# Attention and an MLP mixer on one core: where finished tiles are turned and sent, in the first and in the last batch element

## The chip, the cores and the metric

The kernel runs on one core of one Trainium2 chip. The metric is the device time of one execution in microseconds (us), the median of three runs. A profile of one execution is taken beside it; its span runs from the first to the last instruction.

## The reference

Eight batch elements go through attention with normalised queries and keys (12 heads, 448 tokens, 64 columns a head), and the result of each, 448 tokens by 768 channels, goes through an MLP mixer.

```python
# attention, per head
q_n, k_n = rmsnorm(q, g_q), rmsnorm(k, g_k)
scores = (1 / sqrt(64)) * q_n @ k_n.T
attn = softmax(scores)                      # max taken off, sum + 1e-9
x[b, :, head columns] = attn @ v            # x: (8, 448, 768)
# mixer
h = maximum(x.transpose(0, 2, 1) @ w_tok1, 0) @ w_tok2      # 448 -> 256 -> 448 tokens
u = x + h.transpose(0, 2, 1)
h2 = maximum(u @ w_ch1, 0) @ w_ch2                          # 768 -> 1536 -> 768 channels
out = u + h2                                                # float32
```

The reference computes in float32; the weights can arrive as 64-bit numbers and are converted on the chip.

## The kernel before

One instruction stream is written per engine: the order of the calls is the order on each engine, and an engine waits where its next instruction needs a result or a buffer. The work is cut into small items (a cost in us and a function); `merge` interleaves lists of items by their costs, and `run` emits them. `later(us, fn)` emits `fn` once so many us of item cost have gone by.

The result of an element is kept channel by token (`uT`: six tiles of 128 channels by 448 tokens). To be stored it is turned in blocks of 32 by 32 on VectorE into a tile of `turn_pool` (four buffers), and four transfers, one for each 32 channels, take it to the output:

```python
turn_pool = pool("turn_pool", 4)
r_pool = pool("r_pool", 1)
...
def send_y(b, cc, t):
    dst = out[b][:, cc * P:(cc + 1) * P]
    for i in range(0, P, 32):
        (nc.sync if in_next(b) else nc.scalar).dma_start(
            out=dst[:, i:i + 32].rearrange("(n t) c -> t n c", t=32),
            in_=t[i:i + 32].rearrange("t (n c) -> t n c", c=32))
...
def trans_y(b, cc):
    t = st["y", cc] = turn_pool.tile([P, S], F32, name="turned")
    nc.vector.transpose(out=t[:], in_=st["uT", b][:, cc, :])

def turns(b, cs, send=True):
    def one(cc):
        trans_y(b, cc)
        if send:
            later(2.0, lambda: send_y(b, cc, st.pop(("y", cc))))
    return [(0.3, lambda cc=cc: one(cc)) for cc in cs]

def y_order(b):
    return [o * KC + m for m in ((0, 1, 2) if b else (2, 0, 1)) for o in range(2)]

def in_next(b):                 # this element's tiles are sent inside the next element
    return b < B - 1 and not shifted
```

Element 0 computes the channel MLP in `first_stage` with plain products, 36 stages of 8 matmuls (18 for each layer), while the weights are still being converted on VectorE (`weight_items`: L264, L265, L267, L282, L309) and stored to DRAM. For elements 1 to 7 sums of weight blocks are made on GpSimd (`sum_items`: L205 to L208, loads L241 `raw<-ws`, stores L212 `ws<-raw`), and `ch1` and `ch2` use seven products in place of eight, with weights loaded as units (L740 `unit<-ws`).

```python
def first_stage(n):
    ...
    if t == 0:
        st["m", 0], st["m", 1] = m_tile(), m_tile()        # two PSUM banks, and there are two
    a, u = st.pop(("stage", n)), st["uT", 0]
    for o in range(2):
        ps = st["m", o][:, 0:S]
        ...                                                # matmuls, L781
        if t < last:
            continue
        if wide:                                           # second layer
            to, c = u[:, o * KC + m, :], r_tile(1 + o)[:]
            nc.scalar.copy(out=c, in_=ps)                                    # L790
            nc.gpsimd.tensor_tensor(out=to, in0=to, in1=c, op=ALU.add)       # L791
        else:
            nc.scalar.activation(out=natural(o)[:, :, m, :], ..., func=AF.Relu)
```

Three more places matter. `x_items(0, h)` turns half `h` of element 0's attention result on TensorE (L663) and ScalarE copies it to SBUF (L665); `tok1` multiplies it (L685, with ScalarE's relu L688), `tok2` follows (L693), and VectorE adds its bank to `uT` (L698). Attention for element b+1 runs between these items: scores (L385), exponentials on ScalarE (L389), values (L459), sums (L427), row scales (a square on ScalarE L1170 or L1173, a reduce on VectorE L1187, then L1195 to L1230), and turned queries and keys (L350, L365, L368). The last of the denominators' products with an element's values is L505 on VectorE, its factor turned by L502.

```python
def first_items(tok, prods, some):
    ...
    for j, it in enumerate(prods[:-6]):
        items.append(it)
        ...
        if j in (26, 28):
            items += turns(0, [y_order(0)[j // 2 - 13]])
    return items, prods[-6:]

def last_items(b):
    single = [(us(6, HS), lambda i=i: ch2(b, 1, i, 0)) for i in range(7)]
    l = turns(b, y_order(b)[:4], not in_next(b))
    return [single[0]] + merge(single[1:-1], l) + [single[-1]]
...
for b in range(B):
    early, double = middle_items(b)
    if b == 0:
        early, last = first_items(tok1_items(0, 0) + x_items(0, 1) + tok1_items(0, 1) + early, double, some)
    else:
        if b > 1 and in_next(b - 1):
            y, z = sends(b - 1, y_order(b - 1)[:4]), left
            left = [y[0], y[1], z[0], y[2], z[1], y[3]]
        run(merge(tok1_items(b, 0), left[:2]))
        begin, early = merge(tok1_items(b, 1) + early[:3 * KC], left[2:]), early[3 * KC:]
        ...
    if b == 0:
        last = x_items(1, 1) + merge(last, direct + sums[:5], turns(b, y_order(b)[2:4]))
    else:
        ...
        last += last_items(b)
    run(merge(att, early) + last)
    if b == 0:
        load_units(0)
    left = turns(b, y_order(b)[4:])
run(left)
```

In `ch2` of group 1, the last one, products 0 to 6 (`single`) add into the last channel tiles 2 and 5: tile 2 has its last add at product 5, tile 5's second half at product 4, and tile 5's first half at product 6, the last of all.

Of the kernel before, what the change touches and what calls it, by code (L numbers as in the profile page):

```python
# [8 lines left out]
F32 = mybir.dt.float32  # L9
# [4 lines left out]
ALU = mybir.AluOpType  # L14
# [12 lines left out]
def merge(*lists):  # L27

    totals = [sum(c for c, _ in l) or 1.0 for l in lists]
    done = [0.0] * len(lists)  # L30
    at = [0] * len(lists)
    res = []
    while True:
        live = [i for i in range(len(lists)) if at[i] < len(lists[i])]
        if not live:
            return res
        i = min(live, key=lambda i: (done[i] + lists[i][at[i]][0] / 2) / totals[i])
        c, fn = lists[i][at[i]]
        at[i] += 1
        done[i] += c  # L40
        res.append((c, fn))
# [3 lines left out]
def whole(ctx, tc, shifted, pre, q, k, v, g_q, g_k, moe_w_tok1, moe_w_tok2, moe_w_ch1, moe_w_ch2, out):  # L45


    nc = tc.nc
# [3 lines left out]
    B, H, S, D = q.shape  # L52
# [3 lines left out]
    P = 128  # L56
# [9 lines left out]
    HS = S // 2  # L66
    KC, KF = NC // 2, NF // 2
# [21 lines left out]
    turn_pool = pool("turn_pool", 4)  # L89
# [19 lines left out]
    st = dict(pre.st)  # L109
# [5 lines left out]
    def later(us, fn):  # L115

        at = clock[0] + us
        i = len(pending)
        while i and pending[i - 1][0] > at:
            i -= 1  # L120
        pending.insert(i, (at, fn))

    def run(items):
        for c, fn in items:
            fn()
            clock[0] += c
            while pending and pending[0][0] <= clock[0]:
                pending.pop(0)[1]()
# [496 lines left out]
    def send_y(b, cc, t):  # L625

        dst = out[b][:, cc * P:(cc + 1) * P]
        for i in range(0, P, 32):
            (nc.sync if in_next(b) else nc.scalar).dma_start(
                out=dst[:, i:i + 32].rearrange("(n t) c -> t n c", t=32),  # L630
                in_=t[i:i + 32].rearrange("t (n c) -> t n c", c=32))

# [21 lines left out]
    def trans_x(b, j):  # L654

        half, o = divmod(j, KC)
        if b == 0:

            if o == 0:
                x_tile(b, half)  # L660
            ps = s_tile("t_ps")
            for c in range(NS):
                nc.tensor.transpose(  # L663
                    ps[0:R, c * P:(c + 1) * P], st["uT", b][:, j, c * R:(c + 1) * R], ident[:, :])
            nc.scalar.copy(  # L665
                out=st["x", b, half][0:R, o], in_=ps[0:R, :].rearrange("p (c n) -> p c n", c=NS))
            return

        if j == 0:
            st["xt"] = tu_pool.tile([P, 2, KC, S], F32, name="xt", tag="tu")  # L670
        nc.vector.transpose(out=st["xt"][:, half, o, :], in_=st["uT", b][:, j, :])
        if o == KC - 1:
            t = st["xt"][:, half].rearrange("p j s -> p (j s)")
            if half:
                st.pop("xt")
            later(2.0, lambda: send_x(b, half, t))
            later(12.0, lambda: load_x(b, half))

    def tok1(b, jc, h):
        cs = slice(h * HC, (h + 1) * HC)  # L680
        if h == 0:
            st["h1", jc] = h1_pool.tile([P, C], F32, name="h1", tag="h1")
        ps = m_tile()
        for c in range(NS):
            nc.tensor.matmul(  # L685
                out=ps[:, 0:HC], lhsT=w1_sb[0:R, c, jc * P:(jc + 1) * P], rhs=st["x", b, h][0:R, :, c, :],
                start=(c == 0), stop=(c == NS - 1))
        nc.scalar.activation(out=st["h1", jc][:, cs], in_=ps[:, 0:HC], func=AF.Relu)  # L688
# [63 lines left out]
    def r_tile(i):  # L752
        return r_pool.tile([P, 2 * HS], F32, name=f"r{i}")
# [12 lines left out]
    def natural(o):  # L766
        s = (HB["B11"], HB["T1"]) if o == 0 else (HB["B21"], HB["B22"])
        return hb[:, s[0]:s[1] + 1:s[1] - s[0]]

    def first_stage(n):  # L770

        w, _, m, t = stages[n]
        wide = w is moe_w_ch2
        last = (KF if wide else KC) - 1
        if t == 0:
            st["m", 0], st["m", 1] = m_tile(), m_tile()
# [3 lines that stand above are left out]
            for half in range(2):  # L780
                nc.tensor.matmul(  # L781
                    out=ps, lhsT=a[:, o + 2 * half, :],
                    rhs=natural(half)[:, :, t, :] if wide else u[:, half * KC + t, :],
                    start=(t == 0 and half == 0), stop=(t == last and half == 1))
            if t < last:
                continue
            if wide:

                to, c = u[:, o * KC + m, :], r_tile(1 + o)[:]
                nc.scalar.copy(out=c, in_=ps)  # L790
                nc.gpsimd.tensor_tensor(out=to, in0=to, in1=c, op=ALU.add)  # L791
            else:
                nc.scalar.activation(
                    out=natural(o)[:, :, m, :], in_=ps.rearrange("p (i n) -> p i n", i=2), func=AF.Relu)
        st["used"].add(("stage", n))
# [104 lines left out]
# [9 lines that stand above are left out]
                later(2.0, lambda: send_y(b, cc, st.pop(("y", cc))))  # L909
        return [(0.3, lambda cc=cc: one(cc)) for cc in cs]  # L910

    def y_order(b):

        return [o * KC + m for m in ((0, 1, 2) if b else (2, 0, 1)) for o in range(2)]
# [6 lines left out]
    def x_items(b, h):  # L921
        return [(0.1, lambda j=j: trans_x(b, j)) for j in range(h * NC // 2, (h + 1) * NC // 2)]

    def tok1_items(b, h):
        return [(us(NS, HC), lambda j=j, h=h: tok1(b, j, h)) for j in range(NJ)]
# [13 lines left out]
    def in_next(b):  # L939


        return b < B - 1 and not shifted

    def first_items(tok, prods, some):


        convert = weight_items(BEFORE, len(chunks) + 3)
        items = merge(tok, convert[:5])
        for j, it in enumerate(prods[:-6]):
            items.append(it)  # L950
            items += [(0.0, convert[5 + k][1]) for k in range(len(convert) - 5) if begins(k) == j]
            if j % 2 and j < 2 * len(some):
                items.append(some[j // 2])
            if j in (26, 28):

                items += turns(0, [y_order(0)[j // 2 - 13]])
        return items, prods[-6:]

    def begins(k):
# [4 lines left out]
    def last_items(b):  # L964

        single = [(us(6, HS), lambda i=i: ch2(b, 1, i, 0)) for i in range(7)]
        l = turns(b, y_order(b)[:4], not in_next(b))
        return [single[0]] + merge(single[1:-1], l) + [single[-1]]


# [22 lines left out]
    for p in (4, 5):  # L993
# [7 lines left out]
        out=g_t[:, 0:1], in0=g_t[:, 0:1], scalar=float(D) ** 0.5, in1=g_t[:, 1:2],  # L1001
# [19 lines left out]
    for b in range(B):  # L1021
        early, double = middle_items(b)
        if b == 0:
            early, last = first_items(
                tok1_items(0, 0) + x_items(0, 1) + tok1_items(0, 1) + early, double, some)
        else:
            if b > 1 and in_next(b - 1):

                y, z = sends(b - 1, y_order(b - 1)[:4]), left
                left = [y[0], y[1], z[0], y[2], z[1], y[3]]  # L1030
            run(merge(tok1_items(b, 0), left[:2]))
            begin, early = merge(tok1_items(b, 1) + early[:3 * KC], left[2:]), early[3 * KC:]
            if b == 1:
                early, double = merge(begin + early, sums[5:20]), merge(double, sums[20:])
                begin = []
            early = begin + early + double
            early, last = early[:-4], early[-4:]
        lo = (b + AHEAD) * per + 1
        att = []
        if b + AHEAD < B:  # L1040
            att = att_items(lo, lo + 10) + x_items(b + AHEAD, 0) + att_items(lo + 10, lo + per)
        if b == 0:
            last = x_items(1, 1) + merge(last, direct + sums[:5], turns(b, y_order(b)[2:4]))
        else:
            if b + 1 < B:
                last = merge(last, x_items(b + 1, 1))
            last += last_items(b)
        run(merge(att, early) + last)
        if b == 0:
            load_units(0)  # L1050
        left = turns(b, y_order(b)[4:])
    run(left)
    for _, fn in pending:
        fn()

# [249 lines left out]
```

## Time and profile before

| | |
|---|---|
| time, median of 3 runs (range) | 1345.34 us (1343.76 to 1346.66) |
| span of the profiled run | 1343.4 us |
| mean granted TensorE clock | 0.991 |
| TensorE matmul, busy | 1284.4 us, 96% |
| VectorE, busy | 757.2 us, 56% |
| ScalarE, busy | 368.7 us, 27% |
| GpSimd, busy | 385.1 us, 29% |
| moved by DMA | 227.82 MB, mean 170 GB/s |
| element 1, 272.66 to 435.39 us | 162.73 us, of which TensorE busy 156.68 |
| element 2, 435.39 to 593.00 us | 157.61 us, of which TensorE busy 154.73 |
| from the last add's start to the end | 1333.6 to 1343.4 us |

In the profile PE is TensorE, DVE VectorE, ACT ScalarE, POOL GpSimd and SP SyncE; a q after the name is that engine's sequencer, which issues transfers. L and a number is a line of the kernel. A row of a timeline gives the start and the length in us, the engine, the line, the operation, what is written from what is read, the shapes and the count; in square brackets stands how long the engine was idle before, and what it waited for. A share of busy time is an average: what a change at one place is worth has to be read from the waits at that place.

### The profile page before, as it was taken

To read this page: it belongs to the slowest core of one execution; us is meant where nothing else is said; L and a number is where in the kernel's file an instruction comes from. 1 tells how busy PE (TensorE), PEld (TensorE's weight loads), DVE (VectorE), ACT (ScalarE), POOL (GpSimd) and SP (SyncE) were. 2 spreads that over 40 slices of the span, in tenths; PEclk is the share of its full clock that TensorE was granted. 3 is DMA by queue.
4 is the path that set the end of the run, shared out by engine and by line. 5 is a ranking of instruction groups with operands and counts; after the bars stand their busy time and mean duration, and the time that the engine had idled before them with its cause. 6 is when DMAs were issued, how large, how long until landed. Compare 5 with 4: busy or idle time off the path is not lost.

```text
span 1343.4 us, 20171 instructions
## 1 busy us (share of the span) xinstructions
PE 1284.4 (96%) x7408; PEld 926.5 (69%) x7408; DVE 757.2 (56%) x1289; ACT 368.7 (27%) x740; POOL 385.1 (29%) x449
## 2 busy tenths in 40 slices
PE   5989998989999999999999999999999999999997
PEld 3344444447779477885779667794777867787996
DVE  6887689646764555626664365645556365543212
ACT  5553433123230333212331223302332033300100
POOL 1211540356561223211331222312332033211220
PEclk9999999889999999999999999999999999999998
DMA  9665488889889556794549665594666955476554
GB/s 207 167 170 152 128 221 204 189 234 235 230 204 253 118 154 161 157 223 107 144 117 230 145 153 147 123 254 96 158 158 151 232 119 151 125 189 139 176 172 92
DMA packets 501520, 227.82 MB, mean 170 GB/s; under 512 B 373604, under 2 KB 463076, under 8 KB 501412
## 3 DMA queue, kind: packets, MB, share of 16 engines
q1 hardware_dynamic: 488290, 224.60, 67.9%
q10 hardware_dynamic: 12994, 1.84, 0.8%
q8 instruction: 61, 1.00, 0.3%
q14 instruction: 47, 0.39, 0.1%
q0 software_dynamic: 128, 0.00, 0.0%
HBM read 186.84 MB, written 39.52 MB: 169 GB/s over the span
## 4 chain that ended last, share of the span: by engine, by line
PE 72%; DVE 15%; DMA 4%; POOL 3%; issue 2%; ACT 2%; SPq 1%; DVEq 0%; ACTq 0%; POOLq 0%
PE m_ps L866 25%; PE m_ps L809 19%; PE o_ps L459 7%; PE s_ps L385 7%; PE m_ps L685 5%; PE m_ps L693 4%; DVE es L427 2%; DVE qk_t L350 2%; DMA raw<-in_moe_w_ch_dram 1%; DVE raw L265 1%; DVE raw L282 1%; PE m_ps L781 1%; PE d_ps L439 1%; ACT e L389 1%; DMA unit<-ws 1%
## 5 line engine op out<-in xcount | busy, mean ns | idle before, releaser
L866 PEld LDWEIGHTS m_ps<-hb,unit 128*128 128x128 f32 x1764 | 332.1, 190 | 13.7 <-issue 10.2
L866 PE MATMUL m_ps<-hb,unit 128*128 128x224 f32 x1764 | 339.5, 354 | 0.0
L809 PE MATMUL m_ps<-tu,unit 128*128 128x224 f32 x1008 | 202.6, 355 | 3.8 <-DVE r L814 3.8
L809 PEld LDWEIGHTS m_ps<-tu,unit 128*128 128x128 f32 x1008 | 188.4, 190 | 21.8 <-DVE r L814 7.0
L389 ACT ACTIVATE e<-s_ps 128x448 f32<-128x448 f32 x336 | 157.0, 547 | 99.0 <-PE s_ps L385 98.0
L809 PE MATMUL m_ps<-uT,unit 128*128 128x224 f32 x756 | 154.6, 357 | 6.1 <-ACT r L830 2.5
L385 PE MATMUL s_ps<-qkT 64*64 64x448 f32 x1260 | 147.9, 551 | 9.0 <-ACT qkT L368 4.8
L809 PEld LDWEIGHTS m_ps<-uT,unit 128*128 128x128 f32 x756 | 140.6, 190 | 22.8 <-DVE uT L698 5.7
L459 PE MATMUL o_ps<-e,v 64*64 64x448 f32 x1316 | 150.9, 544 | 0.1
L875 POOL TENSOR_TENSOR uT<-uT,r 128x448 f32<-128x448 f32 (+1 forms) x56 | 52.8, 954 | 263.7 <-DVE r L875 148.9
L814 DVE TENSOR_TENSOR r<-m_ps,r 128x448 f32<-128x448 f32 x63 | 39.0, 619 | 122.5 <-PE m_ps L809 68.3
L875 DVE TENSOR_TENSOR uT<-uT,m_ps 128x448 f32<-128x448 f32 (+1 forms) x70 | 34.1, 503 | 124.5 <-PE m_ps L866 124.5
L427 DVE TENSOR_TENSOR es<-es,e 128x896 f32<-128x896 f32 x84 | 92.6, 1102 | 15.5 <-ACT e L389 12.5
L459 PEld LDWEIGHTS o_ps<-e,v 64*64 64x64 f32 x1316 | 50.9, 134 | 70.6 <-issue 64.6
L385 PEld LDWEIGHTS s_ps<-qkT 64*64 64x64 f32 x1260 | 44.5, 132 | 79.5 <-issue 60.2
L814 POOL TENSOR_TENSOR hb<-r,r 128x448 f32<-128x448 f32 x21 | 27.9, 1327 | 236.0 <-ACT r L830 186.7
L693 PE MATMUL m_ps<-w_sb,h 128*128 128x448 f32 x192 | 80.6, 564 | 7.7 <-DVE uT L698 7.7
L685 PE MATMUL m_ps<-x,w_sb 112*128 112x384 f32 x256 | 86.4, 490 | 1.3 <-ACT x L665 1.0
L368 ACT ACTIVATE qkT<-qkT,g_t 128x448 f32<-128x448 f32 x36 | 24.1, 668 | 214.8 <-DVE qkT L365 214.8
L427 POOL TENSOR_TENSOR es<-e 128x896 f32<-128x896 f32 x21 | 44.1, 2101 | 131.8 <-ACT e L389 131.8
L685 PEld LDWEIGHTS m_ps<-x,w_sb 112*128 112x128 f32 x256 | 47.8, 190 | 37.7 <-ACT e L389 4.2
L1187 DVE TENSOR_REDUCE ms<-sq 128x28 f32<-128x896 f32 (+2 forms) x45 | 48.7, 1084 | 44.4 <-ACT sq L1173 41.8
(117 smaller groups left out, 1378.7 us busy)
## 6 DMA issues: line engine op xcount, KB each, us to landing
unit<-ws SPq DMA_DIRECT2D x294, 384.0 KB, 4.2
raw<-in_moe_w_ch_dram SPq DMA_DIRECT2D x72, 256.0 KB, 3.7
v<-in_v_dram SPq DMA_DIRECT2D x94, 112.0 KB, 4.4
xs<-xt SPq DMA_DIRECT2D x56, 168.0 KB, 4.5
x<-xs SPq DMA_DIRECT2D x14, 672.0 KB, 6.7
out_dram<-turned SPq DMA_DIRECT2D x168, 56.0 KB, 2.0
qk_t<-in_q_dram SPq DMA_DIRECT2D x144, 56.0 KB, 2.7
qk_t<-in_k_dram SPq DMA_DIRECT2D x144, 56.0 KB, 3.7
```

The lines of the kernel that those rows point to most:

```text
L350: nc.vector.tensor_tensor(out=x, in0=x, in1=r.unsqueeze(2).to_broadcast(list(x.shape)), op=ALU.mult)
L385: nc.tensor.matmul(out=pss[i][rows_of(i, a), 0:S], lhsT=qkT[h, 1, k * D:(k + 1) * D], rhs=qkT[h, 0, :], start=True, stop=True)
L389: nc.scalar.activation(out=e[:, i, :], in_=pss[i][:, 0:S], func=AF.Exp)
L427: eng.tensor_tensor(out=es[:], in0=(es if k > 1 else st["e", t, 0])[:], in1=st["e", t, k][:], op=ALU.add)
L459: nc.tensor.matmul(out=st["o", p][a * D:(a + 1) * D, 0:S], lhsT=vt[rows, k * D:(k + 1) * D], rhs=e[rows, :], **kw)
L685: nc.tensor.matmul(out=ps[:, 0:HC], lhsT=w1_sb[0:R, c, jc * P:(jc + 1) * P], rhs=st["x", b, h][0:R, :, c, :], start=(c == 0), stop=(c == N ...
L693: nc.tensor.matmul(out=ps[:, 0:S], lhsT=st["h1", jc][:, cc * P:(cc + 1) * P], rhs=w2_sb[:, jc].rearrange("p c r -> p (c r)"), start=(jc == ...
L809: nc.tensor.matmul(out=ps[:, j * HS:(j + 1) * HS], lhsT=w[:, t, j, :], rhs=m, start=(t == 0), stop=(t == KC - 1))
L814: add = lambda e, o, x, y: e.tensor_tensor(out=o, in0=x, in1=y, op=ALU.add)
L866: nc.tensor.matmul(out=ps[:, j * HS:(j + 1) * HS], lhsT=st["w"](j, t), rhs=hb[:, HB[what], t, :], start=(t == 0), stop=(t == KF - 1))
L875: add = lambda e, o, x, y: e.tensor_tensor(out=o, in0=x, in1=y, op=ALU.add)
L1187: self.nc.vector.tensor_reduce(out=st["ms", p][:, p % 2, lo:hi], in_=sq[:, lo:hi], axis=AX_X, op=ALU.add)
```

## The change

The last element's last two tiles are turned and sent in two parts by tokens, from SyncE's and ScalarE's queues by turns, and its other four tiles are sent from both queues by turns. It is meant to shorten the stretch after the last matmul. In the same step the first element goes another way: VectorE adds the banks of its second layer straight from PSUM, in place of a copy on ScalarE and an add on GpSimd; all of its first four turns stand at its end, and their transfers move into element 1; and the turns of its attention result for half 1 on TensorE stand ahead of `tok1` of half 0.

```diff
 def send_y(b, cc, t):
-            (nc.sync if in_next(b) else nc.scalar).dma_start(
+            (nc.sync if in_next(b) or b == B - 1 and i % (2 * 32) else nc.scalar).dma_start(
 ...
 def first_stage(n):
             if wide:
-                to, c = u[:, o * KC + m, :], r_tile(1 + o)[:]
-                nc.scalar.copy(out=c, in_=ps)
-                nc.gpsimd.tensor_tensor(out=to, in0=to, in1=c, op=ALU.add)
+                to = u[:, o * KC + m, :]
+                nc.vector.tensor_tensor(out=to, in0=to, in1=ps, op=ALU.add)
 ...
+def end_y(cc, halves):
+    for h in halves:
+        t = turn_pool.tile([P, S], F32, name="turned")
+        nc.vector.transpose(out=t[:, 0:HS], in_=st["uT", B - 1][:, cc, h * HS:(h + 1) * HS])
+        dst = out[B - 1][h * HS:(h + 1) * HS, cc * P:(cc + 1) * P]
+        for i in range(0, P, 32):
+            (nc.sync, nc.scalar)[i // 32 % 2].dma_start(
+                out=dst[:, i:i + 32].rearrange("(n t) c -> t n c", t=32),
+                in_=t[i:i + 32, 0:HS].rearrange("t (n c) -> t n c", c=32))
 ...
 def first_items(tok, prods, some):
-            if j in (26, 28):
-                items += turns(0, [y_order(0)[j // 2 - 13]])
 ...
 def last_items(b):
+        if b == B - 1:
+            last = [(0.0, lambda cc=cc, h=h: end_y(cc, h)) for cc, h in ((2, (0, 1)), (KC + 2, (1,)), (KC + 2, (0,)))]
+            return [single[0]] + merge(single[1:-1], l) + last[:2] + [single[-1], last[2]]
         return [single[0]] + merge(single[1:-1], l) + [single[-1]]
 ...
-            early, last = first_items(
-                tok1_items(0, 0) + x_items(0, 1) + tok1_items(0, 1) + early, double, some)
+            early, last = first_items(x_items(0, 1) + tok1_items(0, 0) + tok1_items(0, 1) + early, double, some)
         else:
-            if b > 1 and in_next(b - 1):
+            if in_next(b - 1):
 ...
-            last = x_items(1, 1) + merge(last, direct + sums[:5], turns(b, y_order(b)[2:4]))
+            last = x_items(1, 1) + merge(
+                last, direct + sums[:5], turns(b, y_order(b)[:4], not in_next(b)))
 ...
         left = turns(b, y_order(b)[4:])
-    run(left)
```

## The prediction

> **What bounds the kernel now.** I read the table of engine busy time first: TensorE is busy 1284.4 of 1343.4 us, 96%, and no other engine is above 56%. So only two places can give time back: idle gaps of TensorE, and the stretch after its last matmul. Next the table of waits, for TensorE from 84 to 310 us, where element 0 (the first batch element) is in the MLP and element 1 begins. Columns: who waited, for whom; us in total, times, longest.
>
> ```profile
> PE s_ps L385 <- ACT qkT L368: 4.8, 1, 4.8
> PE s_ps L385 <- ACT x L665: 4.2, 1, 4.2
> PE m_ps L693 <- DVE uT L698: 3.9, 1, 3.9
> PE m_ps L781 <- ACT r L790: 1.6, 1, 1.6
> PE m_ps L685 <- ACT x L665: 1.0, 1, 1.0
> ```
>
> These are all the larger gaps in that stretch, 15.5 us. The timeline places them: 84, 95, 223, 233 and 293 us. Each long one also costs clock: eight L693 matmuls after the gap at 293 took 5.88 us, the eight at 305.5 took 3.27. In the table by stretches, element 1 (272.66 to 435.39 us) lasts 162.73 us and element 2 lasts 157.61: 5.1 us is all that element 1 wastes beyond the steady pattern.
>
> VectorE's waits from 240 to 310 us show what the change was aimed at:
>
> ```profile
> DVE turned L902 <- POOL uT L791: 24.1, 2, 23.6
> ```
>
> VectorE sits 24 us before two turns, until GpSimd adds the last banks. GpSimd's timeline says why that add is late: the ScalarE copies were done at 273.5, but the adds stand behind sums that wait for a load.
>
> ```profile
> 280.45 0.46 POOL L205 TENSOR_TENSOR raw<-raw 128x128 f32<-128x128 f32 x1 [12.40 <-DMA raw<-ws]
> ...
> 284.01 2.23 POOL L791 TENSOR_TENSOR uT<-uT,r 128x448 f32<-128x448 f32 x2
> ```
>
> Behind the turns on VectorE stands the chain that ends in the add L698 (reduce at 286.84, L698 at 295.86), for which TensorE stood 3.9 us. Its last microseconds are in the timelines of VectorE and of ScalarE's queue:
>
> ```profile
> 1333.60 0.39 DVE L875 TENSOR_TENSOR uT<-uT,m_ps 128x224 f32<-128x224 f32 x1 [1.95 <-PE m_ps L866]
> 1333.90 1.16 DVE L902 STREAM_TRANSPOSE turned<-uT 128x448 f32<-128x448 f32 x2
> ```
>
> ```profile
> 1334.94 2.48 ACTq L629 DMA_DIRECT2D out_dram<-turned  x3
> ...
> 1338.96 1.05 ACTq L629 DMA_DIRECT2D out_dram<-turned  x2
> ```
>
> Matmuls end at 1333.5; eight transfers are then issued one after the other until 1340.01; the span ends 3.4 us later. That tail of 9.9 us is bound by issuing on one queue.
>
> **What the Trainium skill says.** "DMA: Bandwidth & Descriptors", section "Issuing engines are not separate DMA queues": starting transfers from several engines saves only sequencer time. Here that is the point: 5.4 us of the tail is issuing. "SBUF — State Buffer", section "SBUF: two separate sides": VectorE and GpSimd share a port pair, locked for a whole instruction. The trace agrees: while L791 ran at 224.63, L282 took 1.62 us and L264 took 1.24, instead of 0.68 and 0.43. "TensorE: Matmul & The Clock Gate", section "What's actually happening": after about 3.4 us idle the array is slow for about 3.4 us; the 5.88 us above agrees.
>
> **The change part by part.**
>
> *Tail.* Four full tiles (16 transfers) go by turns from two queues, then two tiles as four halves (16 transfers of half the size): 16 issues a queue in place of 24 on one. Three halves are turned before the last add. After it remain one half turn (I estimate 0.35 us, half the 0.635 of a full one) and two issues a queue. The add ends at 1333.99, so the last half is ready at 1334.35. Each queue has six half transfers before it from about 1332.1; at 0.5 us each (the median of L629 here) they end at 1335.1, with slot waits 1335.9. The last two end near 1336.5, plus 3.4 us: 1339.4 against 1343.4. **-4.0 us** (between -3 and -5).
>
> *Order of x_items.* The three transposes of half 1 now stand before tok1 of half 0 on TensorE. Their ScalarE copies then no longer stand behind the square at 97.83, so the 4.2 us gap goes. But the built program shows these transposes waiting for VectorE, and the last needs L505's second result, written at 90.14. TensorE now stands from about 84.5 to 90.15: 5.6 us, of which 1.0 was there before. So +4.6, -4.2, and about -0.9 because two of the three transposes run inside the wait; a cold clock follows either gap. **-0.5 us** (±1.5).
>
> *Bank adds.* Six ScalarE copies (529 ns) and six GpSimd adds (1233 ns) go; VectorE gets six adds of about 620 ns. For the first two, VectorE is the limit: it is busy 29.75 of 31.26 us from 210 to 241. The first add stands behind the stretch that ended at 230.45 (now without the 1.75 us lost to the port lock), so TensorE's bank comes free at about 229.4, not 224.6: the gap of 1.6 becomes 6.5. The next wait, for qkT, then nearly vanishes, since it comes from the same VectorE queue: +1.24 for two adds, -1.75 for the lock. **-0.5 us** (±1.5). The other four adds come after 252 us, when VectorE is half idle: 0.
>
> *Sending element 0 late.* All four turned tiles now keep the four buffers of their pool until element 1. The fifth turn needs the first tile's buffer back, and it stands on VectorE before the reduce. The first tile's four transfers stand on SyncE behind seven unit loads. Element 2 shows that pattern, harmless there because the reduce only came at 447:
>
> ```profile
> 442.65 0.65 DVE L902 STREAM_TRANSPOSE turned<-uT 128x448 f32<-128x448 f32 x1 [6.60 <-DMA out_dram<-turned]
> ```
>
> Element 1 has less room: its DMA share is 0.92 from 272 to 310, and the unit loads and transfers there ran like this:
>
> ```profile
> 288.59 1.27 SPq L740 DMA_DIRECT2D unit<-ws  x2
> 289.96 1.55 SPq L629 DMA_DIRECT2D out_dram<-turned  x2
> 292.12 4.06 SPq L629 DMA_DIRECT2D out_dram<-turned  x3
> ```
>
> The four transfers behind the units landed some 11 us after the first unit's issue at 286.07 (issued to 293, 4.3 to land). After the change SyncE has 16 transfers fewer before the units, and GpSimd no adds: I estimate the first unit at 278 to 282. The buffer is then free at 288 to 293, the reduce runs 2 to 6 us later than at 286.84, and L698, about 9 us after it (less if GpSimd locks the port less), comes at 295 to 302. TensorE wants it at 292.6. Its gap of 3.9 becomes 3 to 9: **+2.5 us** (-1 to +5).
>
> Sum: -4.0 - 0.5 - 0.5 + 2.5 = -2.5, so 1345.34 - 2.5 = 1342.8.
>
> **The rivals.** *The old wait goes and none replaces it*: the reduce then follows ScalarE's square at 284.7, 2 us earlier, element 1 loses most of its 5.1 us, and the sum is -8: 1337. The 23.6 us wait speaks for it, the buffer wait in the built program against it. *The buffer wait is long*: 24 transfers and the sums share SyncE, landing later than 293; element 1 loses 8 us or more, the tail's gain is used up: 1347 to 1350. The DMA share of 0.92 speaks for it. *The tail gives little*: if landing and not issuing held the end, two queues save under 1 us: 1346. Against it: 1.7 to 3.7 us from issue to landing.
>
> **Range and chances.** The tail is sure to about 1 us; the first element carries the spread, -4 to +8. I take 1336.5 to 1349. Two per cent is 27 us, more than all gaps named here: within 2% is nearly certain.
>
> **What would show it.** Right: the last transfer issued 3 to 5 us earlier; the L790 and L791 rows gone; no wait of 23 us for GpSimd, but one of VectorE's turn for out_dram near 280 to 293; TensorE waiting near 85 us for VectorE and near 223 for the L789 adds; no long wait at 233; elements 2 to 6 at 157.6 us each. Wrong: if element 1 comes down to about 158 us, or rises above 168, or if the waits at 85 or 223 us, which I placed by queue order, cost several us more than the gaps they replace.

## The result

The changed kernel takes 1351.82 us (median of four runs, 1351.66 to 1352.05) against 1345.62 us for the kernel before in four runs: a ratio of 1.0048, with a 95% interval of 1.0030 to 1.0065. It is about 6 us slower, where I had expected 2.5 us less. The profiled span grew from 1343.4 to 1350.2 us.

Before any reason is looked for, the span is cut where TensorE begins a new element (its first matmul on line L685):

| stretch | before, us | after, us | difference | predicted |
|---|---|---|---|---|
| start to element 1 | 272.66 | 273.29 | +0.6 | -1.0 |
| element 1 | 162.73 | 169.56 | +6.8 | +2.5 |
| elements 2 to 7, to the last matmul | 898.1 | 898.1 | 0 | 0 |
| after the last matmul | 9.9 | 9.2 | -0.7 | -4.0 |

The last element was the aim of the change and gave 0.7 us. Element 1, which only receives transfers that element 0 used to send, lost ten times that.

The table of waits of the changed kernel, TensorE's and VectorE's, from 240 or 272 to 320 us (who waited, for whom; us in total, times, longest), shows what took the place of the 23.6 us wait for GpSimd and of the 3.9 us wait for L698:

```profile
PE m_ps L693 <- ACT h L688: 7.4, 1, 7.4
```

```profile
DVE turned L900 <- DMA out_dram<-turned: 21.7, 1, 21.7
DVE uT L789 <- PE m_ps L781: 11.0, 3, 9.8
```

VectorE still stands 21.7 us before a turn, now for a transfer to the output: the fifth turned tile needs one of the four buffers back. How that reaches TensorE can be followed through four timelines of the same kernel (start, length, engine, line, operation; in brackets the idle time before and what ended it), those of SyncE's queue, VectorE, ScalarE and TensorE:

```profile
283.62 3.60 SPq L740 DMA_DIRECT2D unit<-ws  x7
287.31 8.04 SPq L629 DMA_DIRECT2D out_dram<-turned  x8
```

```profile
295.79 0.65 DVE L900 STREAM_TRANSPOSE turned<-uT 128x448 f32<-128x448 f32 x1 [21.68 <-DMA out_dram<-turned]
296.36 1.04 DVE L1196 TENSOR_REDUCE ms<-sq 128x28 f32<-128x896 f32 x1
```

```profile
297.44 1.01 ACT L1204 COPY half<-ms 32x56 f32<-32x56 f32 x4 [12.04 <-DVE ms L1196]
298.47 0.49 ACT L688 ACTIVATE h<-m_ps 128x384 f32<-128x384 f32 x1
```

```profile
299.02 7.33 PE L693 MATMUL m_ps<-w_sb,h 128*128 128x448 f32 x12 [7.38 <-ACT h L688]
```

Element 0's first tile leaves SyncE only after seven unit loads. It has landed at 295.8; then VectorE turns and reduces, ScalarE copies the reduce's result (four copies), and only behind these copies, in ScalarE's order, stands the relu that TensorE wants. None of these steps takes over 1.04 us; the order hands the wait on. "TensorE: Matmul & The Clock Gate" of the Trainium skill, section "What's actually happening", has the array slow again after idling, and this gap agrees: the twelve matmuls after it took 7.33 us, where eight with no gap before them took 3.27 in the kernel before (at 305.51), which would be 4.9 for twelve. The page gives at least one busy stretch of about 3.4 us before full speed returns; here the granted clock was 0.50 from 299.0 to 304.0, so for 5 us.

In the tail of the changed kernel, VectorE and the two queues (the row at 1342.24 is one of the eight of SyncE's queue above it):

```profile
1339.03 0.99 DVE L914 STREAM_TRANSPOSE turned<-uT 128x224 f32<-128x224 f32 x3
1339.46 6.25 SPq L917 DMA_DIRECT2D out_dram<-turned  x8
1340.38 5.70 ACTq L917 DMA_DIRECT2D out_dram<-turned  x8
...
1342.24 1.79 SPq L917 DMA_DIRECT2D out_dram<-turned  x1
...
1342.36 0.41 DVE L914 STREAM_TRANSPOSE turned<-uT 128x224 f32<-128x224 f32 x1 [0.91 <-DMA out_dram<-turned]
```

The matmuls end at 1340.96. Three halves are turned before that, as planned, and the last half waits 0.91 us for a buffer. But that wait doesn't set the end: the half is turned at 1342.77, and the queues come to its transfers only at 1344.9. On each queue one earlier issue takes 1.8 us, until 1344.0, where the median is 0.44; what it waits for, the profile doesn't show. So each queue needs some 6 us for eight half transfers (6.25 / 8 = 0.78 us each, no less than the 16.79 / 24 = 0.70 of a whole tile's transfer before). The last issue ends 5.1 us after the last matmul (6.5 before), and the span ends 4.1 us after it (3.4 before); this stretch holds the last landing and some 2.0 us more in both kernels.

### The profile page after: what moved, and what is told of

Its sections match the earlier page's. It is cut to its first block, busy times and chain, and to the rows that moved or that the text cites. A ratio compares the mean times of both kernels' runs of the same rounds, so it can differ in the third digit from the quotient of the medians.

```text
span 1350.2 us, 20175 instructions
## 1 busy us (share of the span) xinstructions
PE 1286.4 (95%) x7408; PEld 924.7 (68%) x7408; DVE 753.7 (56%) x1297; ACT 365.6 (27%) x734; POOL 379.8 (28%) x443
## 4 chain that ended last, share of the span: by engine, by line
PE 70%; DVE 16%; DMA 6%; issue 2%; ACT 2%; POOL 2%; SPq 2%; DVEq 0%; ACTq 0%; POOLq 0%
PE m_ps L864 23%; PE m_ps L807 19%; PE s_ps L385 7%; PE o_ps L459 7%; PE m_ps L685 5%; PE m_ps L693 3%; PE m_ps L781 3%; DVE es L427 2%; DVE qk_t L350 2%; DMA unit<-ws 2%; PE d_ps L439 1%; ACT e L389 1%; DMA raw<-in_moe_w_ch_dram 1%; DVE raw L265 1%; DVE qkT L365 1%
## 5 line engine op out<-in xcount | busy, mean ns | idle before, releaser
L864 PEld LDWEIGHTS m_ps<-hb,unit 128*128 128x128 f32 x1764 | 332.1, 190 | 14.3 <-issue 10.8
L807 PE MATMUL m_ps<-tu,unit 128*128 128x224 f32 x1008 | 202.8, 356 | 4.0 <-DVE r L812 3.8
L807 PEld LDWEIGHTS m_ps<-tu,unit 128*128 128x128 f32 x1008 | 188.3, 190 | 23.0 <-DVE r L812 6.2
L807 PE MATMUL m_ps<-uT,unit 128*128 128x224 f32 x756 | 155.0, 357 | 6.3 <-ACT r L828 3.1
L807 PEld LDWEIGHTS m_ps<-uT,unit 128*128 128x128 f32 x756 | 140.4, 190 | 23.2 <-DVE uT L698 7.0
L385 PE MATMUL s_ps<-qkT 64*64 64x448 f32 x1260 | 145.1, 547 | 0.2 <-ACT qkT L368 0.2
L693 PE MATMUL m_ps<-w_sb,h 128*128 128x448 f32 x192 | 80.7, 564 | 12.1 <-ACT h L688 7.4
L685 PE MATMUL m_ps<-x,w_sb 112*128 112x384 f32 x256 | 88.8, 501 | 0.3 <-DMA x<-xs 0.3
L685 PEld LDWEIGHTS m_ps<-x,w_sb 112*128 112x128 f32 x256 | 48.9, 194 | 37.4 <-issue 4.5
L693 PEld LDWEIGHTS m_ps<-w_sb,h 128*128 128x128 f32 x192 | 35.7, 195 | 53.8 <-issue 24.5
```

Source lines behind the costliest of these rows:

```text
L385: nc.tensor.matmul(out=pss[i][rows_of(i, a), 0:S], lhsT=qkT[h, 1, k * D:(k + 1) * D], rhs=qkT[h, 0, :], start=True, stop=True)
L685: nc.tensor.matmul(out=ps[:, 0:HC], lhsT=w1_sb[0:R, c, jc * P:(jc + 1) * P], rhs=st["x", b, h][0:R, :, c, :], start=(c == 0), stop=(c == N ...
L693: nc.tensor.matmul(out=ps[:, 0:S], lhsT=st["h1", jc][:, cc * P:(cc + 1) * P], rhs=w2_sb[:, jc].rearrange("p c r -> p (c r)"), start=(jc == ...
L807: nc.tensor.matmul(out=ps[:, j * HS:(j + 1) * HS], lhsT=w[:, t, j, :], rhs=m, start=(t == 0), stop=(t == KC - 1))
L864: nc.tensor.matmul(out=ps[:, j * HS:(j + 1) * HS], lhsT=st["w"](j, t), rhs=hb[:, HB[what], t, :], start=(t == 0), stop=(t == KF - 1))
```

## The experiments

All times are medians beside the kernel before on the same chip, which had medians of 1346.1 to 1346.6. The ratios and their 95% intervals come from all the runs and can differ a little from the quotient of two medians. Runs of one kernel spread over several us, some of it in the stretch up to element 1 (272.1 to 274.2 us in four traces of kernels with the same first element), so the stretches are read from the traces and the verdicts from the intervals.

### The parts one at a time

**The tail alone**, put into the kernel before.

```diff
+def end_y(cc, halves): ...        # as in the change
 def send_y(b, cc, t):
-            (nc.sync if in_next(b) else nc.scalar)
+            (nc.sync if in_next(b) or b == B - 1 and i % (2 * 32) else nc.scalar)
 def last_items(b):
+        if b == B - 1: ...            # as in the change
```

> The kernel before with the tail of the change alone (sends of the last element from two queues by turns, its last two tiles turned and sent as four halves); the first element as before. Theory 'the tail gives little because the halves are as many transfers again and wait for one another to land': last matmul at 1333.5 us, end of span 9.2 us after it, so 1345.5 - 0.7 = about 1344.8. Rival, the prediction's term of -4.0: 1341.5. If the tail had a hidden cost for the first element too, it would be above 1346.

Measured: 1345.80 us, ratio 0.9992 (0.9982 to 1.0002). From the last matmul to the end 9.2 us against 9.9. In time the tail is worth 0.4 us by the medians and 1.1 by the ratio. No change at all lies within the interval, the 4 us that were predicted lie outside it. So the tail had no large gain that another part took away.

**The late transfers alone**: element 0's four turns at its end, sent in element 1.

```diff
-            if j in (26, 28):
-                items += turns(0, [y_order(0)[j // 2 - 13]])
-            if b > 1 and in_next(b - 1):
+            if in_next(b - 1):
-            last = x_items(1, 1) + merge(last, direct + sums[:5], turns(b, y_order(b)[2:4]))
+            last = x_items(1, 1) + merge(last, direct + sums[:5], turns(b, y_order(b)[:4], not in_next(b)))
```

> The kernel before with one part of the change: element 0's first four turns at its end, their transfers inside element 1. Bank adds still on ScalarE and GpSimd, x_items and tail as before. Theory 'late sending alone costs element 1': element 1 about 168 to 170 us, time 1350 to 1353. Rival 'it is the adds on VectorE or the order of x_items that made element 1 longer': element 1 stays at 162.7, time 1345 to 1346.

Measured: 1355.51 us, ratio 1.0075 (1.0049 to 1.0102), more than was expected; element 1 lasts 172.0 us, 9.3 more than before. VectorE's wait, from 240 to 320 us in its trace, is there without any other part of the change:

```profile
DVE turned L902 <- DMA out_dram<-turned: 34.1, 1, 34.1
```

**The bank adds alone**, on VectorE.

```diff
-                to, c = u[:, o * KC + m, :], r_tile(1 + o)[:]
-                nc.scalar.copy(out=c, in_=ps)
-                nc.gpsimd.tensor_tensor(out=to, in0=to, in1=c, op=ALU.add)
+                to = u[:, o * KC + m, :]
+                nc.vector.tensor_tensor(out=to, in0=to, in1=ps, op=ALU.add)
```

> The kernel before with the bank adds alone moved to VectorE, straight from PSUM; turns and sends of element 0 early as before. Theory: GpSimd's late add no longer holds VectorE's turns (23.6 us wait gone), the reduce follows the square near 285 us, element 1 falls to about 158 to 160 us; the gap near 223 us grows to some 8 us and the one at 233 nearly goes, about +0.5 net; time 1341 to 1343. Rival 'something else in element 1 holds TensorE, such as the loads of units': element 1 stays near 162.7, time about 1346.

Measured: 1344.03 us, ratio 0.9985 (0.9971 to 0.9998). The profile says how it comes about. Element 1 lasts 157.6 us (275.95 to 433.57), so that all of its 5.1 us of waste is gone, and TensorE's wait before L693 falls from 3.90 to 0.28 us. But element 1 starts 3.3 us later, and the wait that I had placed near 223 us came, as long as predicted, and a second behind it. TensorE's timeline of this kernel:

```profile
230.08 8.02 PE L781 MATMUL m_ps<-hb,stage 128*128 128x448 f32 x16 [6.79 <-DVE uT L789]
256.11 20.00 PE L781 MATMUL m_ps<-hb,stage 128*128 128x448 f32 x48 [2.62 <-DVE uT L789]
...
295.71 3.27 PE L693 MATMUL m_ps<-w_sb,h 128*128 128x448 f32 x8 [0.28 <-DVE uT L698]
```

Both effects are in all four traces of the kernel before with these adds (two of them with a changed tail, below): element 1 lasts 156.5 to 158.3 us, against 162.7 to 163.2 in the four without them. Its start is less sure, 272.9 to 277.2 against 272.1 to 274.2, on average 2 us later.

**The same adds again**, on the chip on which the tails below were run.

> The kernel before with the bank adds on VectorE alone, on the same chip as the two others. If its gain is what it was (2.2 us): 1343.5 to 1344.5. If the chip or the run-to-run spread of element 1 gave the larger gains of the kernels with both: 1340 to 1342.5.

Measured: 1342.62 us, ratio 0.9969 (0.9959 to 0.9979), element 1 158.3 us. The gain lies between my two figures; the adds are worth 2 to 4 us.

**The order of x's items alone.**

```diff
-first_items(tok1_items(0, 0) + x_items(0, 1) + tok1_items(0, 1) + early, double, some)
+first_items(x_items(0, 1) + tok1_items(0, 0) + tok1_items(0, 1) + early, double, some)
```

> The kernel before with only the order of x's items changed (second half's loads of x ahead of the token products' items). My step put -0.5 us on it: 1345.1 to 1345.9 against 1346. Rival (the new order is a part of the loss): +1 us or more, element 0 reaches element 1 later than 272.7 us.

Measured: 1346.48 us, ratio 1.0004 (0.9992 to 1.0015): nothing. (What moves are the turns of x on TensorE, not loads.) In its trace element 1 begins at 274.59, later than 272.7 as the rival said, but lasts only 160.4 us.

By medians the four parts add up: -0.4 + 9.3 - 2.2 (or -4.0) + 0 = +6.7 (or +4.9), against +6.2 measured for the whole.

### The changed kernel without the late transfers

```diff
 # the changed kernel, with the turns at j in (26, 28), y_order(b)[2:4] and "b > 1" put back
```

> The changed kernel, with element 0's four tiles turned and sent early again, as before. Theory (the late sends cost the whole excess): 1341.5 to 1344 us, that is 1346 less some 2 for the bank adds on VectorE and 0.6 for the tail; element 1 begins its products near 272 us and lasts 161 to 163. Rival (the loss comes from the parts together, the adds or the order of x's items included): over 1347, and element 1 still lasts over 166.

Measured: 1341.02 us, ratio 0.9964 (0.9946 to 0.9983); element 1 lasts 158.0 us. So the transfers' move costs the changed kernel 10.8 us by the medians (11 by the ratios), and without it the rest of the change is a gain. The rival, an interplay of parts, falls.

### Which property of the late transfers costs

**More buffers.** Element 0's fifth and sixth turned tiles go into two free tiles of `r_pool`, so that no turn waits.

```diff
-        t = st["y", cc] = turn_pool.tile([P, S], F32, name="turned")
+        spare = b == 0 and cc in y_order(0)[4:]
+        t = st["y", cc] = r_tile(3 + 2 * (cc // KC)) if spare else turn_pool.tile([P, S], F32, name="turned")
```

> The changed kernel, but the fifth and sixth turned tile of element 0 go into two tiles of r_pool that stand idle then, and no longer wait for a turn buffer; the 24 late transfers stay on SyncE as they are. Theory 'the buffer wait cost element 1 its 6.8 us': VectorE's wait of 21.7 us for out_dram goes, its reduce follows ScalarE's square near 285.5 us, TensorE's 7.4 us wait goes, element 1 falls from 169.6 to about 159 to 161 us, time 1342 to 1344. Rival 'the late transfers crowd SyncE and the DMA queues whatever the buffers do': element 1 stays above 166 us, time about 1350.

Measured: 1349.88 us, ratio 1.0026 (1.0013 to 1.0039). The 7.4 us gap is gone and the first product of the channel MLP (L807) comes at 303.98 us in place of 313.10. Yet element 1 ends at 442.62 in place of 442.85: the 9 us are lost again on the way, and the rival holds. The second loss is not one gap but many. The longest of TensorE's waits from 300 to 443 us:

```profile
PE m_ps L864 <- DMA unit<-ws: 2.0, 1, 2.0
PE m_ps L807 <- DVE hb L812: 1.9, 1, 1.9
PE o_ps L459 <- DMA v<-in_v_dram: 1.4, 1, 1.4
PE m_ps L807 <- ACT r L816: 1.2, 1, 1.2
```

and ScalarE's timeline says why a mere copy from PSUM (L816) is late:

```profile
336.37 0.95 ACT L1183 ACTIVATE sq<-qk_t 128x896 f32<-128x896 f32 x1 [9.65 <-DMA qk_t<-in_k_dram]
338.47 1.00 ACT L1205 COPY half<-ms 32x56 f32<-32x56 f32 x4 [1.15 <-DVE ms L1197]
339.49 0.58 ACT L813 ACTIVATE hb<-hb 128x448 f32<-128x448 f32 x1
339.98 0.51 ACT L816 COPY r<-m_ps 128x448 f32<-128x448 f32 x1
```

The square waits 9.65 us for keys of the next attention; the copy stands behind the square. SyncE's timeline of the same run shows where the keys' load stands, behind the last of element 0's transfers (309.40) and all that follows them; it lands 4.1 us after it is issued:

```profile
309.40 2.26 SPq L629 DMA_DIRECT2D out_dram<-turned  x4
...
331.60 0.95 SPq L1164 DMA_DIRECT2D qk_t<-in_k_dram  x2
```

In the changed kernel the same load is issued at 330.44, hardly earlier, but no square waits for it: there ScalarE comes to that square only at 335.75. So the two limits stand side by side, the buffer on the one and SyncE's queue on the other, nearly equal in length, and the later one sets the time.

**The same transfers with less data**: with the spare buffers, each of element 0's 24 transfers carries 2 of its 14 blocks (the rest of element 0's output is left unwritten).

```diff
+            few = 2 if b == 0 else S // 32
-                out=dst[:, i:i + 32].rearrange("(n t) c -> t n c", t=32),
-                in_=t[i:i + 32].rearrange("t (n c) -> t n c", c=32))
+                out=dst[:, i:i + 32].rearrange("(n t) c -> t n c", t=32)[:, 0:few],
+                in_=t[i:i + 32].rearrange("t (n c) -> t n c", c=32)[:, 0:few])
```

> The changed kernel with the spare buffers for element 0's last two turned tiles, and each of element 0's 24 transfers to the output cut to a seventh of its data (2 of 14 blocks of 32 tokens; the rest of element 0's output is left unwritten). The number of issues stays. Theory A (the transfers' own work, 448 pieces of 128 bytes each, takes the DMA's time in element 1): element 1 ends near 436 us in place of 442.6 and the time is 1342 to 1345. Theory B (24 issues stand ahead of the weight loads in SyncE's queue, in order): under 1.5 us is won, 1348 to 1350.

Measured: 1347.45 us, ratio 1.0014 (1.0002 to 1.0025). Between the two theories: six sevenths of the data are worth about 2 us (from 1.0026 to 1.0014; the intervals overlap). The square's wait is 6.9 us still. In the one trace element 1 ends at 435.64, which was theory A's sign, and lasts 163.8 us in place of 168.7; but that run, 1344.88 us, was the fastest of twelve, so the medians decide.

**Fewer transfers**: with the spare buffers, element 0's first three tiles are turned but not sent (left unwritten), so that SyncE has 12 transfers in element 1, as before.

```diff
         dst = out[b][:, cc * P:(cc + 1) * P]
+        if b == 0 and cc in y_order(0)[:3]: return
```

> The changed kernel with the spare buffers, and with element 0's first three tiles turned as before but never sent: 12 of its 24 transfers fall away, issue and data both, so that SyncE has as many of them in element 1 as in the kernel before (three tiles of the output are left unwritten). Theory B (SyncE's queue in order: what was put ahead of the loads for attention and weights): 1341 to 1344, 4 us or more under the 1347.5 of the run whose transfers were thin; element 1 lasts 161 to 164. Rival C (the turns' new places in the list of element 1's work have moved other engines' work too, so that PE waits whatever is sent): still 1346 to 1349.

Measured: 1343.45 us, ratio 0.9983 (0.9972 to 0.9995). Element 1 lasts 160.4 us. SyncE comes to the end of element 0's transfers 10.2 us earlier (299.24 for 309.40), and to the same load of keys 9.7 us earlier:

```profile
299.24 2.17 SPq L630 DMA_DIRECT2D out_dram<-turned  x4
...
321.86 1.04 SPq L1165 DMA_DIRECT2D qk_t<-in_k_dram  x2
```

The square nearly finds its keys, as ScalarE's timeline shows:

```profile
327.13 0.95 ACT L1184 ACTIVATE sq<-qk_t 128x896 f32<-128x896 f32 x1 [0.83 <-DMA unit<-ws]
```

(The row names a load of weights, but the keys' two loads are issued at 321.9 and 322.3 and land 4.6 to 4.8 us later, the last at 326.9, just before the square.)

Twelve transfers fewer give about 6 us against the run with spare buffers alone, and 4.0 against the run where all 24 are there but thin. The 24 thin transfers carry less data than these 12, and are slower. So most of the second loss hangs on the transfers' number in SyncE's queue, the lesser part on their data. The turns stay at their new places here, so that rival C, which blamed these, keeps at most the 2.4 us left to the kernel without the late transfers.

**The transfers from ScalarE's queue**, with the spare buffers.

```diff
-            (nc.sync if in_next(b) or b == B - 1 ...
+            (nc.sync if in_next(b) and b > 0 or b == B - 1 ...
```

> The changed kernel with the spare buffers, and element 0's 24 late transfers issued from ScalarE's queue in place of SyncE's. The data is the same. Theory A (the DMA's time): 1348 to 1351, element 1 ends after 441 us. Theory B (SyncE's order): element 1 ends near 436 and the time is 1342 to 1345, unless ScalarE, which then waits ahead of its relus, loses some of it.

Measured: 1362.90 us, ratio 1.0119 (1.0102 to 1.0136), worse than either theory. It doesn't tell them apart: TensorE now waits 7.9 us for x, and ScalarE's own work stands behind the transfers. From ScalarE's waits, 270 to 330 us:

```profile
ACT e L389 <- DMA out_dram<-turned: 10.6, 1, 10.6
```

Here the engine that issues also computes, and its exponentials stand 10.6 us until transfers ahead of them are issued. Whether the plain time of SyncE's issues sets the second loss, or what makes some of them longer (0.48 to 1.91 us for the first eight in the changed kernel), is therefore not separated. Nor was it tried to issue the same 24 transfers on SyncE behind the loads, which would part their order from their number.

### Where the tail's gain went

Two queues with six whole tiles, and the same with tile 2 turned and sent ahead of the last product. Both without the other parts, then both with the bank adds.

```diff
 # (1) two queues
-            (nc.sync if in_next(b) else nc.scalar)
+            (nc.sync if in_next(b) or b == B - 1 and i % (2 * 32) else nc.scalar)
 # (2) besides, in last_items, and without run(left) at the end:
+        if b == B - 1:
+            def now(cc):
+                trans_y(b, cc)
+                send_y(b, cc, st.pop(("y", cc)))
+            return [single[0]] + merge(single[1:-1], l) + [(0.0, lambda: now(2)), single[-1], (0.0, lambda: now(KC + 2))]
```

> The kernel before with only the last element's six whole tiles sent by turns from both queues. Theory (halves took the gain: twice the transfers, and a turn that waits for a buffer): 8 to 8.8 us from the last product to the end, and 1344 to 1345 us, 1.0 to 1.8 under before. Rival (the gain seen with the adds came from the adds and the chip): 1345.5 to 1346.5, no better than the tail with halves.

> The kernel before with both queues and whole tiles, and the second-last tile turned and sent ahead of the last product. Theory: 6.4 to 7 us from the last product to the end, 1342 to 1343.5 us, 3 to 4 under before. Rival: over 1344.5.

> The kernel before with the bank adds on VectorE, and the last element's six full tiles sent by turns from both queues, no halves, order of the tail else as before. Theory (transfers in flight and landings set the pace of the tail, not the issues): from the last product to the end 9.5 to 10 us against 9.9 before and 9.2 with halves; time 1343 to 1344.5. Rival (one queue's issues were the bound, and only the doubling of transfers ate the gain): 7 us or less from the last product, 1341 to 1342.

> The same, with the second-last tile turned and sent whole ahead of the last product, so that after the last product one whole tile is left, four transfers, two on each queue. If the number of transfers after the last product is what costs: 6.5 to 8 us from the last product to the end and 1341 to 1342.5. If landing and the last turn set it: 8.5 to 9.5 us, 1343 to 1344.

| tail | last matmul to last issue | to the end | time, us | ratio (interval) |
|---|---|---|---|---|
| before: whole tiles, one queue | 6.5 | 9.9 | | |
| halves, two queues (alone) | 5.3 | 9.2 | 1345.80 | 0.9992 (0.9982 to 1.0002) |
| (1) whole tiles, two queues | 4.0 | 8.8 | 1344.36 | 0.9989 (0.9981 to 0.9998) |
| (2) besides, tile 2 early | 2.1 | 6.8 | 1343.67 | 0.9970 (0.9958 to 0.9982) |
| (1) with the bank adds | 3.9 | 8.6 | 1339.70 | 0.9954 (0.9940 to 0.9968) |
| (2) with the bank adds | 2.2 | 6.6 | 1337.79 | 0.9942 (0.9925 to 0.9960) |

The first two columns are from one trace each; the rows were not all run on one chip. In the traces whole tiles beat halves by 0.4 us, which the times can't tell apart. The early tile is worth 2.0 us more in the traces, and the times agree, with intervals that touch: in (2) without the adds, four transfers are left once tile 5's last add is done.

```profile
1333.29 0.65 DVE L902 STREAM_TRANSPOSE turned<-uT 128x448 f32<-128x448 f32 x1
1335.21 0.39 DVE L875 TENSOR_TENSOR uT<-uT,m_ps 128x224 f32<-128x224 f32 x1 [1.27 <-PE m_ps L866]
1335.63 0.65 DVE L902 STREAM_TRANSPOSE turned<-uT 128x448 f32<-128x448 f32 x1
```

In this trace VectorE's timeline shows tile 2 whole at 1333.29, tile 5 after the add, and no turn that waits for a buffer. The matmuls end at 1335.10, and the last issue at 1337.24.

For the two kernels with the adds I had expected too little. 1344.36 less the adds' 2 to 4 us is 1340.4 to 1342.4, and 1339.70 was measured: the spread of the adds' gain covers most of it, and under 1 us stays unexplained. **The last row beats both kernels**: 1337.79 us, 8.3 less than the kernel before beside it (7.8 by the ratio) and some 14 less than the changed one, which was run on another occasion. What it takes of the change is the bank adds and the two queues; it leaves the halves, the late transfers and the order of x's items.

## Why the prediction was wrong, by its own steps

**What bounds the kernel.** Right. Only gaps of TensorE and the stretch after it could move the time; elements 2 to 7 took 898.1 us in both traces. The slow clock was put at about 3.4 us; in the kernel before, too, it was 0.50 for 5 us (296.5 to 301.5).

**Sending element 0 late.** This is the step that failed. Its mechanism was right as far as the reduce: seven unit loads, then the first tile's transfers, then the buffer, the turn, the reduce. The first unit was issued at 283.6, where I had put 278 to 282 as an estimate, and the buffer came 12 us after it, near the 11 I had read; so the reduce came at 296.36, 9.5 us later than before, where I had said 2 to 6. From there the path was another one. I had TensorE wait for the add L698, about 9 us after the reduce. It waited for the relu L688, which stood behind the reduce's copies on ScalarE and ended at 298.96; L698 came at 301.10, 4.7 us after the reduce, and TensorE didn't wait for it there. That the gap of 7.4 us lay within the 3 to 9 named is luck, a later reduce and a shorter path.

What failed most is the sum drawn from it, +2.5 us. Against the changed kernel without the late transfers, element 1 grew from 158.0 to 169.56, by 11.6. First, I compared the gap with the kernel before's 3.9 us, and left out that the adds alone remove that gap (to 0.28); so the whole 7.4 is loss, and the slow clock behind it costs about 7.33 - 4.9 = 2.4 more. Together 9.8, which is most of 11.6. Second, I looked at one limit where there are two side by side. With the buffers' wait taken away, the same transfers came out as late keys and late units, and element 1 ended no earlier. The rival "the buffer wait is long" came nearest. Element 1 lost 6.8 us against the kernel before, where the rival had 8 or more, but 11.6 by the comparison that counts; the time of 1351.82 us lies above its 1347 to 1350. The reason that it gave, 24 transfers sharing SyncE, is the second limit. Each limit by itself was not priced: no run has the 12 transfers fewer with the four buffers.

**The tail.** The second step that failed, by 3.3 us: from the last matmul 5.9 us were predicted and 9.2 measured. A half transfer was taken to be a cheap one of 0.5 us, with 0.8 us on each queue for waits. Its median issue is 0.44 us, but with the waits it is 0.71 to 0.78, and on each queue a single issue took 1.8 us: the issues ended 5.1 us after the last matmul and not 3.0. From the last issue to the end it took 4.1 and not 3.4. (And the sum on record was 0.5 us short in itself: 1336.5 plus 3.4 is 1339.9.) "DMA: Bandwidth & Descriptors", section "Issuing engines are not separate DMA queues", with its saving of sequencer time alone, is what (1) shows: issuing ends 6.5 - 4.0 = 2.5 us sooner, but 1.4 of that is given back from there to the end, which comes 4.8 us after the last issue against 3.4. The rival "the tail gives little" was right on the size; its reason, that landing holds the end, is half of it, for (2) ends 2.0 us sooner than (1) with nearly the same stretch behind the last issue, 4.7 us against 4.8.

**The bank adds.** The wait at the first adds came where predicted, with 6.8 and 8.7 us in the two runs where 6.5 was said; a second one behind it, of 2.6 and 1.0 us, was not foreseen. Element 1 began some 2 us later, where -0.5 was said. And "the other four adds: 0" was wrong in the good direction: with no wait for GpSimd, the turns, the reduce and L698 came in time, and element 1 lost all its 5.1 us of waste. That was in the rival "the old wait goes and none replaces it", and it is true of the adds by themselves. Net -2 to -4.

**The order of x's items.** -0.5 predicted, +0.5 (-1.1 to +2.0) measured. The wait near 85 us for VectorE came, and the one at 95 us went, as predicted.

## What to carry to other kernels

Work that is moved off a stretch where it hurt takes its buffers and its place in the queue along: list what stands behind it there on every in-order engine, and price each, for removing the first wait may only uncover the second. A gap should be compared with what the other parts of the same change would leave, not with the gap before. At a kernel's end, count the transfers that are issued after the last result: fewer and earlier ones gained here, and more and smaller ones gained hardly anything.

## What was not expected of the hardware

Halving a transfer from 56 to 28 KB hardly changed its landing in the changed kernel's tail: medians 2.6 and 2.7 us for whole tiles, 2.4 and 3.0 for halves, on SyncE's and ScalarE's queue. With two queues at work the landing grew instead, from a median of 2.0 us for the last 24 transfers on one queue (kernel before) to 3.2 and 3.8 us on SyncE's and ScalarE's in the fastest kernel, with whole tiles in both.
